# Between two expert layers: where the next layer's statistics, low parts and first rows are made

## The chip, the cores and the metric

One core of one Trainium2 chip runs the whole program. The metric is the device time of one execution in microseconds (us), as a median of several runs. Lines named L... are lines of the kernel before, as the profile names them.

## What is computed

A decaying linear attention over 3,072 tokens makes 384 numbers for each token, and two layers of experts follow. Each layer has 8 experts and sends every token to one of them; the second layer also has a capacity, which drops tokens past it.

```python
logits = x @ w_gate                      # first layer: + modality_bias[modality_id]
e_idx = argmax(logits, 1)                # one expert for each token
gate = 1 / sum(exp(logits - max))        # weight of the chosen expert
out[e_idx == e] = gate * (relu(x @ w1[e]) @ w2[e])
```

Here x is 3072x384, w1[e] is 384x1024 and w2[e] is 1024x384. The second layer routes the first layer's output, so it cannot gather a row before the last token of the first layer has its logits.

## The kernel before

**Places.** Tokens are sorted by expert and cut into places of 128 rows. With this input the first layer has 26 places (0 to 25) and the second 28. Place `j` works in lane `j % 2`, and each lane keeps one expert's matrices: the raw float32 (`raw[l][m]`, m = 0 for w1, 1 for w2), a float16 high part `hi` and a bfloat16 low part `lo`, both scaled by a power of two that follows from the matrix's sum of squares.

**One place.** `fetch` gathers 128 rows by an indirect DMA that GpSimd issues; `turn` transposes them on TensorE. `up` makes the first products (72 matmuls), `hidden` the Relu and its low part, `down` the second products (24 matmuls, the last 8 with the low part of the hidden rows). `record`, `gate` and `chance` make a first-layer row's float16 pair, its second-layer logits and its gate; `store` writes it by GpSimd.

**A new matrix.** ScalarE or VectorE sums its squares in three pieces (`gauge`, L964 on ScalarE, L966 on VectorE), `total` (L970, L971) adds the pieces, `tally` (L907) is a matmul that sums over partitions, `scale` (L917 to L919) makes the power of two, `cast` (L876) or `prep` (L981) makes the high part on ScalarE, and `rest` (L880) or `prep` (L983) the low part on VectorE.

**The order of the work.** Every engine's instructions stand in the order in which the code below issues them; no scheduler moves them. `weave` takes turns between generators. The number of places is known only at run time, so the last steps are nested `If`s on the register `used`, and each has an `Else` with a copy of `drain`, the code for the last place. `drain(25)` runs here. Its bits for place 25 (a new second matrix, a short run of an expert) are not set. An `If` costs the engines in it a branch, and at its end they bring their semaphores to one value; an engine outside it that reads what was written there waits for that end.

**drain(25) before.** It starts with three squares of `raw[0][0]` (`size[0]`), then `up(25)`, `hidden(25)`, then `finish(25)`, whose branch for this input makes three more squares of `raw[0][0]` and two of `raw[1][0]`, woven with the record and gate of earlier places. `down(24)` calls `tally` ahead of its last 8 matmuls (key `2 * KF`), which waits for the end of `finish`. After the second products of 24 and 25 come the last logits, `recall` (it brings each token's choice from places back to token order), `scale` and `cast(0, 0)`, the counting of the second layer's experts (`count_all`, `order`, `sizes`, `places`), and beside it `slow_rest(0, 0)`: four times a multiply and a subtract of 512 columns on GpSimd (L992, L993), which make the low part of two thirds of `raw[0][0]`. Then the engines leave the nest, and `first(1)` compares, multiplies and gathers the first rows of the second layer (`choice` L1055 and L1056, `rows` L1061 to L1065, `check`, `fetch_` L1090, `write`). The flag `redo` is read by four engines (L1702), and `slots(1)` starts with the last third of `raw[0][0]` (`rest(0, 0, 2)`), the table of runs, `turn(0)`, `cast(1, 0)` and `rest(1, 0)`.

Of the kernel before, what the change touches and what calls it, by code (L numbers as in the profile page):

```python
# [11 lines left out]
FP32 = mybir.dt.float32  # L12
# [11 lines left out]
P = 128  # L24
# [75 lines left out]
class Kernel:  # L100
# [774 lines left out]
        for r, h, w in self.thirds(l, m):  # L875
            self.nc.scalar.activation(out=h, in_=r, func=ACTF.Copy, scale=self.wsc[l][m][:, 0:1])  # L876

    def rest(self, l, m, i=0):
        for r, h, w in self.thirds(l, m)[i:]:
            self.nc.vector.scalar_tensor_tensor(  # L880
                out=w, in0=r, scalar=self.wsc[l][m][:, 0:1], in1=h, op0=ALU.mult, op1=ALU.subtract
            )
# [38 lines left out]
    def experts(self, ctx):  # L921
# [34 lines left out]
        def gauge(l, m, i=0, j=3, wait=0, e=S):  # L956

            r, sq = flat(raw[l][m]), self.sq[:, l, m]
            for k in range(wait):
                yield  # L960
            for k in range(i, j):
                x = r[:, k * F:(k + 1) * F]
                if e is S:
                    S.activation(out=junk[:, 0:F], in_=x, func=ACTF.Square, accum_out=sq[:, k:k + 1])  # L964
                else:
                    stt_(out=junk1[:, 0:F], in0=x, scalar=1.0, in1=x, op0=ALU.mult, op1=ALU.mult, accum_out=sq[:, k:k + 1])  # L966
                yield
# [11 lines left out]
        def prep(l, m):  # L979
            for r, h, w in self.thirds(l, m):  # L980
                S.activation(out=h, in_=r, func=ACTF.Copy, scale=wsc[l][m][:, 0:1])  # L981
                yield
                stt_(out=w, in0=r, scalar=wsc[l][m][:, 0:1], in1=h, op0=ALU.mult, op1=ALU.subtract)  # L983

        tmp = [xp.tile([P, F // 2], FP32, name=f"tmp{i}") for i in range(2)]

        def slow_rest(l, m):

            for r, h, w in self.thirds(l, m):
                for i in range(2):  # L990
                    f = slice(i * F // 2, (i + 1) * F // 2)
                    G.tensor_tensor(out=tmp[i], in0=r[:, f], in1=wsc[l][m][:, 0:1].to_broadcast([P, F // 2]), op=ALU.mult)  # L992
                    G.tensor_tensor(out=w[:, f], in0=tmp[i], in1=h[:, f], op=ALU.subtract)  # L993
                    yield

        def inverse(l):
            V.tensor_tensor(out=winv[l], in0=wsc[l][0][:, 1:2], in1=wsc[l][1][:, 1:2], op=ALU.mult)
# [219 lines left out]
        def slots(layer, banks):  # L1217
# [277 lines left out]
            def step(t):  # L1495
# [43 lines left out]
                do(logits, t - 3)  # L1539
                do(turn_rows, t - 2)  # L1540

            def drain(t):
                if layer == 0:
                    size = [gauge((t - 1) % 2, 0), gauge(t % 2, 0, 2), chain(gauge((t - 1) % 2, 1), gauge(t % 2, 1))]
                    weave(islice(size[0], 3))
                up(t)
                hidden(t)
                finish(t, False, (lambda: gauge(t % 2, 0, 0, 2, 3)) if layer == 0 else lambda: ())
                down(t - 1, {2 * KF: tally})
                weigh(t)  # L1550
                renew(t, False)
                load(t, 1)
                if layer == 1:
                    for j in (t - 1, t):
                        if j == t:
                            down(t)
                        weave(out(j))
                        store(j, ob[j % 4][:, 0:D])
                    return
                rec = [record(j) for j in (t - 1, t)]  # L1560
                prob = [chance(j, j > t - 2) for j in range(t - 3, t + 1)]
                slow = slow_rest(0, 0)

                def settled(j):
                    weave(prob[j - t + 3])
                    store(j, ob[j % 4])

                def between():
                    logits(t - 2)
                    logits_plain(t - 1, t)  # L1570

                plain(t - 1)
                turn_out(t - 2)
                logits(t - 3)
                next(rec[0])
                weave(gate(t - 3))
                down(t, {KF: lambda: turn_plain(t - 1), 2 * KF: between})
                next(size[1])
                next(prob[0])
                next(rec[0])  # L1580
                next(rec[0])
                settled(t - 3)
                weave(gate(t - 2), gate(t - 1, plain_logits(t - 1, t)))
                plain(t)
                for l in range(2):
                    total(l, 0)
                weave(rec[0])
                turn_plain(t)
                next(prob[1])
                next(prob[2])  # L1590
                next(rec[1])
                recall(0, t, mk[0], gm, 32)
                tally()
                logits_plain(t, t)
                weave(gate(t, plain_logits(t, t)), prob[1], prob[2])
                store(t - 2, ob[(t - 2) % 4])
                store(t - 1, ob[(t - 1) % 4])
                next(rec[1])
                next(rec[1])
                next(prob[3])  # L1600
                recall(t, t + 1, mk[1], gl, 4)
                for l in range(2):
                    scale(l, 0)
                self.cast(0, 0)
                weave(islice(size[2], 2))
                V.tensor_tensor(out=mk[0], in0=mk[0], in1=mk[1], op=ALU.max)
                V.tensor_tensor(
                    out=self.oh.rearrange("p t e -> p (t e)").rearrange("p (e t) -> p e t", t=NT),
                    in0=C["rev"].rearrange("p (t e) -> p e t", e=NE), in1=mk[0].unsqueeze(1).to_broadcast([P, NE, NT]), op=ALU.is_equal,
                )  # L1610
                self.count_all(pm)
                weave(rec[1])
                weave(islice(slow, 2))
                onehot = self.order(sm, pm, 0, NT, 9, True)
                weave(islice(onehot, 5), sizes(True), prob[3])
                store(t, ob[t % 4])
                weave(islice(slow, 2))
                weave(onehot, places(True))
                weave(size[2])

            def some(n):
                weave(islice(todo, n))
# [3 lines left out]
            if layer == 0:  # L1626
                todo = runs(False)
                choice(SOON, NS)
                rows(SOON, NS)
                write(SOON, NS)  # L1630
                weave(halve(0))
                turn(0)
                weave(halve(1))
            else:
                self.rest(0, 0, 2)
                todo = runs(True)
                some(23)
                load(0, 0)
                turn(0)
                for l in range(2):  # L1640
                    total(l, 1)
                self.cast(1, 0)
                self.rest(1, 0)
                load(1, 0)

# [13 lines left out]
                with c.Else():  # L1659
                    drain(t)  # L1660

            used = reg(2, A, D_, PE, PL, SP)
            last(sure)

        def begin(layer):
# [32 lines left out]
        banks = hs, ys, xtp, otp, lgp  # L1698
        with tc.manual_schedule():
            slots(0, banks)  # L1700
            first(1)
            x = nc.values_load(redo, engines=[ET.Activation, ET.DVE, ET.PE, ET.SP], min_val=0, max_val=1)  # L1702
            with tc.If(x):
                afresh(1)
            slots(1, banks)
# [63 lines left out]
```

## Time and profile before

| | us |
|---|---|
| median of 3 runs (1004.43 to 1015.93) | 1006.25 |
| profiled execution, its own time | 1013.21 |
| its span, first to last instruction | 1011.2 |
| TensorE busy | 784.3 |
| VectorE busy | 713.4 |
| ScalarE busy | 563.7 |
| GpSimd busy | 132.7 |
| TensorE's mean granted clock, share of full speed | 0.872 |

Busy times are sums over the whole program. The change touches some 60 us of it, from the start of the first layer's last place to the second layer's first steps, so what counts is the order of events there: for each engine when an instruction started, how long it sat idle before, and what ended that.

### The profile page before, as it was taken

The page shows a single profiled execution, that of the slowest core. Times are in us where ns is not written, and L with a number is a line of the kernel's source. Part 1 is how long each engine was busy: PE and PEld are TensorE (multiplying, and loading weights), DVE is VectorE, ACT ScalarE, POOL GpSimd, SP SyncE. Part 2 cuts the span into 40 slices and gives each one's busy share as a digit, 9 for nine tenths or more (in the row PEclk, how much of TensorE's full clock was granted, in tenths as well). Part 3 has the DMA queues.
Part 4 walks back from the last instruction along what each step waited for, and adds up shares of the span by engine and source line. Part 5 has one row for each costly group of instructions (what it writes and reads, how often), then busy time and mean ns, then how long its engine had stood idle before and what let it go on. Part 6 is the DMA issues. An engine that isn't in the chain of part 4 may idle for free. (4 is left out here: it accounts for less than half of the span.)

```text
span 1011.2 us, 24545 instructions
## 1 busy us (share of the span) xinstructions
PE 784.3 (78%) x8691; PEld 630.1 (62%) x8691; DVE 713.4 (71%) x2694; ACT 563.7 (56%) x1066; POOL 132.7 (13%) x137
## 2 busy tenths in 40 slices
PE   4343237999899969568799999867177999989994
PEld 2111115888788858456688888745065787768872
DVE  6899998999999897757656656643887556774220
ACT  6455346777656685148655555555656666773221
POOL 1000000000000000200122222110521232222211
PEclk9665557999999968688999999977588999999998
DMA  4211111222222631273261111150064354331110
GB/s 114 106 53 54 58 53 53 81 87 91 75 96 65 238 138 48 52 266 97 68 231 52 51 52 51 35 154 13 26 232 155 104 175 162 109 98 47 49 44 28
DMA packets 49155, 95.06 MB, mean 94 GB/s; under 512 B 14377, under 2 KB 33479, under 8 KB 48913
## 3 DMA queue, kind: packets, MB, share of 16 engines
q1 hardware_dynamic: 36864, 70.89, 20.5%
q0 software_dynamic: 7312, 21.40, 6.9%
q8 instruction: 79, 1.29, 0.6%
q14 instruction: 164, 1.34, 0.4%
q10 hardware_dynamic: 4736, 0.14, 0.3%
HBM read 211.92 MB, written 20.11 MB: 229 GB/s over the span
## 5 line engine op out<-in xcount | busy, mean ns | idle before, releaser
L1278 PE MATMUL hs<-xt,h 128*128 128x128 f16 x2592 | 227.0, 226 | 17.4 <-issue 8.1
L1278 PEld LDWEIGHTS <-h 128*128 128x128 f16 x2592 | 173.0, 101 | 22.8 <-issue 11.7
L1278 PE MATMUL hs<-xt,l 128*128 128x128 f16 x1296 | 149.6, 226 | 4.4 <-DVEq L1439 2.7
L1295 PE MATMUL ys<-cums,hh 128*128 128x384 bf16 (+1 forms) x864 | 150.5, 327 | 0.0
L248 PE MATMUL tp<-sq,ct 128*128 128x432 f32 (+3 forms) x92 | 60.7, 812 | 82.0 <-ACT sq L244 74.1
L1287 DVE SCALAR_TENSOR_TENSOR hl<-hs,hh 128x512 bf16<-128x512 f32 x108 | 70.7, 685 | 68.3 <-ACT hh L1284 67.0
L1295 PEld LDWEIGHTS <-hh 128*128 128x128 f16 x864 | 82.7, 98 | 49.7 <-issue 1.2
L1278 PEld LDWEIGHTS <-l 128*128 128x128 bf16 x1296 | 95.1, 101 | 5.9 <-DVEq L1439 3.3
L1284 ACT ACTIVATE hh<-hs 128x512 f16<-128x512 f32 x108 | 60.7, 589 | 63.3 <-PE hs L1278 59.1
L248 PEld LDWEIGHTS tp<-sq,ct 128*128 128x128 f32 x92 | 24.0, 290 | 114.2 <-ACT sq L244 92.7
L291 DVE TENSOR_TENSOR u<-cums,nz 128x108 f32<-128x108 f32 (+1 forms) x381 | 86.8, 252 | 5.3 <-ACT nz L266 3.4
L1295 PE MATMUL ys<-cums,hl 128*128 128x384 f16 x432 | 84.1, 340 | 0.0
L1090 POOL DMA_INDIRECT xg<-rec,rd x58 | 57.2, 986 | 152.8 <-issue 56.4
L1295 PEld LDWEIGHTS <-hl 128*128 128x128 bf16 x432 | 39.6, 100 | 53.2 <-issue 30.6
L298 DVE TENSOR_TENSOR cums<-u 128x54 f32<-128x54 f32 (+1 forms) x381 | 68.3, 203 | 2.5 <-DVE u L291 0.2
L964 ACT ACTIVATE junk<-cums 128x1024 bf16<-128x1024 f32 x54 | 56.9, 1054 | 20.5 <-DMA cums<-in_w 11.8
L397 PE MATMUL tp<-ct,qk 128*112 128x128 f32 x384 | 60.1, 293 | 6.0 <-DVE qk L391 5.6
L435 PE MATMUL sc<-qT,kT 112*128 112x128 f32 x384 | 53.7, 288 | 2.3 <-ACT qT L400 2.3
L397 PEld LDWEIGHTS tp<-ct,qk 128*112 128x112 f32 x384 | 45.3, 143 | 12.9 <-DVE qk L391 6.6
L1241 POOL DMA_INDIRECT rec<-ob,wr x26 | 26.0, 1002 | 207.7 <-ACTq L1434 137.7
L1011 POOL MEMSET thr<- 1x2 f32 x1 | 0.1, 90 | 397.0 <-PE tp L397 397.0
L435 PEld LDWEIGHTS sc<-qT,kT 112*128 112x128 f32 x384 | 48.8, 200 | 5.0 <-ACT qT L400 3.1
(328 smaller groups left out, 1630.7 us busy)
## 6 DMA issues: line engine op xcount, KB each, us to landing
cums<-in_w SPq DMA_DIRECT2D x112, 1536.0 KB
qkv<-in_qkvt SPq DMA_DIRECT2D x24, 576.0 KB
nz<-in_ain SPq DMA_DIRECT2D x20, 432.0 KB
rec<-xs SPq DMA_DIRECT2D x24, 192.0 KB
out<-zero SPq DMA_DIRECT2D x24, 192.0 KB
xg<-rec,rd POOLq DMA_INDIRECT x58, 3.6
ct<-in_consts POOLq DMA_DIRECT2D x1, 524.5 KB, 5.8
out<-ob,wr POOLq DMA_INDIRECT x28, 3.2
```

The lines of the kernel that those rows point to most:

```text
L248: nc.tensor.matmul(m2, ident, sq[:, r], start=(r == 0), stop=(r == 1))
L291: V.tensor_tensor(out=u, in0=rep(f[:, 1, e - 1, x], S_), in1=four(z[:, 1, k * X + c * w:k * X + (c + 1) * w], s_), op=ALU.mult)
L298: ins = V.tensor_tensor(out=two(f[:, 1, e, x], S_), in0=u[:, :, 0], in1=u[:, :, 1], op=ALU.add)
L397: nc.tensor.transpose(tp[:112, hh * P:(hh + 1) * P], src[:, g * 4 + hh].rearrange("p r d -> p (r d)")[:, :112], ident)
L435: nc.tensor.matmul(sc[:, hh], kT[:, h], qT[:, h], start=True, stop=True)
L964: S.activation(out=junk[:, 0:F], in_=x, func=ACTF.Square, accum_out=sq[:, k:k + 1])
L1090: G.indirect_dma_start(out=xg[j % 3], out_offset=None, in_=self.rec[layer], in_offset=bass.IndirectOffsetOnAxis(ap=rd[:, j:j + 1], axis=0))
L1241: G.indirect_dma_start(out=dst, out_offset=bass.IndirectOffsetOnAxis(ap=wr[:, j:j + 1], axis=0), in_=x, in_offset=None, bounds_check=N - 1 ...
L1278: T.matmul(hs[q][:, g], m[:, c, f], x[:, o + c], start=(n == 0), stop=(n == 3 * KD - 1))
L1284: S.activation(out=hh[j % 2][:, sl], in_=h, func=ACTF.Relu)
L1287: V.scalar_tensor_tensor(out=hl[j % 2][:, sl], in0=h, scalar=0.0, in1=hh[j % 2][:, sl], op0=ALU.max, op1=ALU.subtract)
L1295: T.matmul(y, h[j % 2][:, g], m[:, g], start=(n == 0), stop=(n == 3 * KF - 1))
```

## The change

It edits `drain`, the last place of either layer, and what follows the first layer. `finish`, `weigh` and `renew` are replaced there: `finish_last` has one `If` (a new second matrix) and no squares, and stands behind `up`; a second `If` on the new register `short`, in which TensorE takes part as well, stands behind `down(t - 1)`, which calls no `tally`. The six squares of the two first matrices stand ahead: three behind `finish_last`, three behind `hidden` and ahead of `plain(t - 1)`. `tally` goes into `down(t)` at `KF + 4`, `scale` and `cast(0, 0)` behind it, `rest` of two thirds of `raw[0][0]` goes to VectorE, and `slow_rest` is removed. `cast(1, 0)` moves from the second layer's start to the place where `cast(0, 0)` was, and `first(1)` from behind the nest to the end of each `drain`.

```diff
             def drain(t):
                 if layer == 0:
-                    size = [gauge((t - 1) % 2, 0), gauge(t % 2, 0, 2), chain(gauge((t - 1) % 2, 1), gauge(t % 2, 1))]
-                    weave(islice(size[0], 3))
+                    size = [gauge((t - 1) % 2, 0), gauge(t % 2, 0), chain(gauge((t - 1) % 2, 1), gauge(t % 2, 1))]
                 up(t)
+                finish_last(t)
+                if layer == 0:
+                    weave(size[0])
                 hidden(t)
-                finish(t, False, (lambda: gauge(t % 2, 0, 0, 2, 3)) if layer == 0 else lambda: ())
-                down(t - 1, {2 * KF: tally})
-                weigh(t)
-                renew(t, False)
+                down(t - 1)
+                with when(short, t):
+                    weave(measure(t % 2, 1))
+                    tally()
+                    scale(t % 2, 1)
+                    weave(prep(t % 2, 1))
+                    inverse(t % 2)
                 load(t, 1)
...
+                weave(size[1])
                 plain(t - 1)
...
-                down(t, {KF: lambda: turn_plain(t - 1), 2 * KF: between})
-                next(size[1])
+                for l in range(2):
+                    total(l, 0)
+                down(t, {KF: lambda: turn_plain(t - 1), KF + 4: tally, 2 * KF: between})
                 next(prob[0])
                 next(rec[0])
                 next(rec[0])
-                settled(t - 3)
+                for l in range(2):
+                    scale(l, 0)
+                self.cast(0, 0)
+                self.rest(0, 0, 0, 2)
+                weave(prob[0])
+                store(t - 3, ob[(t - 3) % 4])
                 weave(gate(t - 2), gate(t - 1, plain_logits(t - 1, t)))
                 plain(t)
-                for l in range(2):
-                    total(l, 0)
...
-                tally()
                 logits_plain(t, t)
...
-                for l in range(2):
-                    scale(l, 0)
-                self.cast(0, 0)
-                weave(islice(size[2], 2))
+                self.cast(1, 0)
+                weave(islice(size[2], 1))
...
-                weave(islice(slow, 2))
                 onehot = self.order(sm, pm, 0, NT, 9, True)
                 weave(islice(onehot, 5), sizes(True), prob[3])
                 store(t, ob[t % 4])
-                weave(islice(slow, 2))
                 weave(onehot, places(True))
                 weave(size[2])
+                first(1)
...
+            def finish_last(t):
+                def rows_(*more):
+                    weave(*more, out(t - 2), *([chain(gate(t - 4), chance(t - 4))] if layer == 0 else []))
+                with when(bits[0], t) as c:
+                    rows_(prep(t % 2, 1))
+                    inverse(t % 2)
+                with c.Else():
+                    rows_()
...
-            used = reg(2, A, D_, PE, PL, SP)
+            used, short = reg(2, A, D_, PE, PL, SP), reg(1, A, D_, PE)
```

In the second layer's `slots`, `cast(1, 0)` is left out ahead of `rest(1, 0)`.

TensorE's order in `drain(25)`, kernel before, from the last of the first 16 second products of place 24 on (`hh` is the high part of the hidden rows, `hl` the low part):

```order
L1295 LDWEIGHTS hh_4733
L1295 MATMUL ys_5519<-cums,hh_4733 128x384
L1473 UNCONDITIONAL_BRANCH
L907 LDWEIGHTS onesb
L907 MATMUL m<-sqb,onesb 128x4 [waits DVE_49]
L1295 LDWEIGHTS hl_4735
L1295 MATMUL ys_5519<-cums,hl_4735 128x384
```

The same place with the change, from the last second product of place 24:

```order
L1284 LDWEIGHTS hl_4735
L1284 MATMUL ys_5517<-cums,hl_4735 128x384
L1557 REGISTER_ALU
L1557 COMPARE_AND_BRANCH
L907 LDWEIGHTS onesb
L907 MATMUL m<-sqb,onesb 128x4 [waits DVE_49]
L1557 UNCONDITIONAL_BRANCH
L1557 UNCONDITIONAL_BRANCH [waits PE_49]
L1316 LDWEIGHTS ob_4740 [waits Activation_49]
```

The sum matmul that waits for VectorE no longer stands inside the second products; a branch on `short` stands behind them, and the matmul in it is skipped when the bit is not set.

GpSimd's order at the end of `drain(25)`, kernel before (`rec` is the table of rows that the second layer gathers from):

```order
L992 TENSOR_TENSOR tmp_4760<-cums,wsc_294 128x512
L993 TENSOR_TENSOR l_0_3900<-tmp_4760,h_0_3899 128x512 [waits PE_49,Pool_49]
L1765 ISA [waits DMASW7_49]
L1241 DMA rec_63<-ob_4738,wr 3072x385 [waits DMASW7_49,DMASW6_49,DVE_49]
L992 TENSOR_TENSOR tmp_4759<-cums,wsc_294 128x512
L993 TENSOR_TENSOR l_0_3900<-tmp_4759,h_0_3899 128x512 [waits Activation_49,Pool_49]
```

With the change:

```order
L1230 DMA rec_63<-ob_4737,wr 3072x385 [waits DMASW5_49,DVE_49,Activation_49]
L1770 ISA [waits DMASW7_49]
L1230 DMA rec_63<-ob_4738,wr 3072x385 [waits DMASW6_49,DMASW7_49,DVE_49,Activation_49]
L1770 ISA [waits DMASW0_49]
L1079 DMA xg_4722<-rec_63,rd 128x385 [waits DMASW7_49,DMASW1_49,DVE_49]
L1662 ISA [waits DMASW2_49,DMASW1_49]
L1662 UNCONDITIONAL_BRANCH
```

The multiplies and subtracts are gone, and the second layer's first gather stands ahead of the branch out of the nest.

VectorE's last rows in `drain(25)`, kernel before (`bt` is each token's place):

```order
L824 TENSOR_TENSOR ro<-iota_268,rr 128x384
L1044 TENSOR_TENSOR bt<-bt,ov 128x24 [waits DVE_49]
L1047 TENSOR_SCALAR x_4768<-bt,l_4767 128x24 [waits DVE_49]
L1049 SCALAR_TENSOR_TENSOR bt<-bt,x_4768 128x24 [waits DVE_49]
L1656 UNCONDITIONAL_BRANCH
```

With the change `so` and `sv` of `choice` and the five rows of `check` stand behind the same three rows of `bt`, and then:

```order
L1053 TENSOR_SCALAR gz<-m 128x6 [waits PE_49]
L1054 TENSOR_TENSOR rd<-m,gz 128x6 [waits DVE_49]
L1059 TENSOR_SCALAR em<-m 128x6
L1060 TENSOR_TENSOR em<-em,gz 128x6 [waits DVE_49]
L1061 TENSOR_TENSOR wr<-m,em 128x6 [waits DVE_49]
L1662 UNCONDITIONAL_BRANCH
```

The branch out of the nest stood between `bt` and the rows made from it; now it stands behind them.

## Rows read from the trace of the kernel before

**Rows 1.** Busy time of each engine in one stretch, with clock and DMA.

```profile
core 0: us, PE busy (x) PEld busy (x) DVE busy (x) ACT busy (x) POOL busy (x), PEclk, DMA share, GB/s
...
712.00:727.30 15.30, 0.81 (x3) 0.31 (x3) 14.78 (x30) 13.45 (x25) 11.85 (x10) 0.50 0.11 41
```

**Rows 2.** Timeline, TensorE: start, length, line, operation, [idle before, and what ended it].

```profile
682.34 0.48 PE L1278 MATMUL hs<-xt,h 128*128 128x128 f16 x3 [4.28 <-issue]
...
687.74 2.93 PE L1295 MATMUL ys<-cums,hh 128*128 128x384 f16 x16
696.70 0.16 PE L907 MATMUL m<-sqb,onesb 128*128 128x4 bf16 x1 [6.03 <-DVE ob L1385]
...
704.62 1.46 PE L1295 MATMUL ys<-cums,hl 128*128 128x384 f16 x8
...
707.14 0.75 PE L1404 MATMUL hs<-marks,roT 128*128 128x25 f16 x24
```

**Rows 3.** Timeline, ScalarE, from the hidden rows of place 25 to the counting.

```profile
688.89 1.06 ACT L964 ACTIVATE junk<-cums 128x1024 bf16<-128x1024 f32 x1 [0.31 <-ACT hh L1284]
...
690.77 1.06 ACT L964 ACTIVATE junk<-cums 128x1024 bf16<-128x1024 f32 x1
...
691.95 1.06 ACT L964 ACTIVATE junk<-cums 128x1024 bf16<-128x1024 f32 x1
...
699.48 0.58 ACT L1341 ACTIVATE xs<-ys,fx 128x384 f32<-128x384 f32 x1 [3.41 <-PE ys L1295]
...
706.12 0.58 ACT L1341 ACTIVATE xs<-ys,fx 128x384 f32<-128x384 f32 x1 [1.15 <-PE ys L1295]
...
711.68 3.23 ACT L876 ACTIVATE h<-cums,wsc 128x1024 f16<-128x1024 f32 x3 [0.30 <-DVE wsc L918]
...
718.82 2.73 ACT L818 ACTIVATE ab<-iota,rr 128x128 f16<-128x128 f16 x9 [1.69 <-DVE rr L813]
721.58 1.16 ACT L819 ACTIVATE ro<-ab 128x1152 f16<-128x1152 f16 x1
```

**Rows 4.** Timeline, VectorE, from the last gates to the second layer's start.

```profile
705.00 0.16 DVE L1363 COPY g<-lgp 128x8 f32<-128x8 f32 x1
...
706.08 0.16 DVE L1373 TENSOR_REDUCE marks<-g 128x1 f16<-128x8 f32 x1
...
711.31 0.15 DVE L917 TENSOR_SCALAR wsc<-m 128x1 int32<-128x1 int32 x1
...
711.93 0.17 DVE L1606 TENSOR_TENSOR mk<-mk,mk 128x24 f32<-128x24 f32 x1
...
714.47 0.23 DVE L1019 TENSOR_SCALAR sl<-m,cap 128x8 f32<-128x8 f32 x1 [0.27 <-PE m L1017]
...
714.94 1.50 DVE L1021 TENSOR_SCALAR sl<-sl 128x8 f32<-128x8 f32 x1
...
725.81 1.19 DVE L1047 TENSOR_SCALAR x<-bt,l 128x24 f32<-128x24 f32 x1
...
729.84 0.32 DVE L1055 TENSOR_TENSOR so<-iota,bt 128x144 f16<-128x144 f16 x1 [2.62 <-issue]
...
733.32 1.28 DVE L880 SCALAR_TENSOR_TENSOR l<-cums,wsc,h 128x1024 bf16<-128x1024 f32 x1 [1.12 <-DVEq L1703]
```

**Rows 5.** Timeline, VectorE, the first layer's own counting, GpSimd idle beside it.

```profile
411.00 0.17 DVE L837 TENSOR_SCALAR sl<-sl 128x8 f32<-128x8 f32 x1
...
412.69 0.24 DVE L1047 TENSOR_SCALAR x<-bt,l 128x24 f32<-128x24 f32 x1
```

**Rows 6.** Timeline, GpSimd: the second layer's first gather.

```profile
732.01 1.01 POOL L1090 DMA_INDIRECT xg<-rec,rd  x1 [5.04 <-DVE em L1071]
```

**Rows 7.** Branches on the number of places, TensorE's sequencer: ns min/median/max, times.

```profile
L1656 PEldq COMPARE_BRANCH  x10: 66/76/4822, 646.4 to 993.8; - x10
```

**Rows 8.** Timeline, TensorE, the second layer's first transposes and first sum.

```profile
736.07 0.82 PE L1267 MATMUL xtp<-ident,xg 128*128 128x128 f16 x6 [4.73 <-DVE cb L1143]
...
753.64 0.16 PE L907 MATMUL m<-sqb,onesb 128*128 128x4 bf16 x1 [0.74 <-DVEq L1517]
```

More of the change, by code (lines that the diff above doesn't have):

```diff
@@ L876, in cast, with rest @@
             self.nc.scalar.activation(out=h, in_=r, func=ACTF.Copy, scale=self.wsc[l][m][:, 0:1])
-    def rest(self, l, m, i=0):
-        for r, h, w in self.thirds(l, m)[i:]:
+    def rest(self, l, m, i=0, j=3):
+        for r, h, w in self.thirds(l, m)[i:j]:
             self.nc.vector.scalar_tensor_tensor(
@@ L983, in prep @@
                 stt_(out=w, in0=r, scalar=wsc[l][m][:, 0:1], in1=h, op0=ALU.mult, op1=ALU.subtract)
[L985 to L994, printed above, removed]
         def inverse(l):
@@ L1540, in step @@
                 do(turn_rows, t - 2)
+            def finish_last(t):
[6 more added lines that the diff above has]
+                    rows_()
+                if layer == 1:
+                    store(t - 2, ob[(t - 2) % 4][:, 0:D])
+                else:
+                    store(t - 4, ob[(t - 4) % 4])
             def drain(t):
                 if layer == 0:
-                    size = [gauge((t - 1) % 2, 0), gauge(t % 2, 0, 2), chain(gauge((t - 1) % 2, 1), gauge(t % 2, 1))]
-                    weave(islice(size[0], 3))
+                    size = [gauge((t - 1) % 2, 0), gauge(t % 2, 0), chain(gauge((t - 1) % 2, 1), gauge(t % 2, 1))]
                 up(t)
+                finish_last(t)
+                if layer == 0:
+                    weave(size[0])
                 hidden(t)
-                finish(t, False, (lambda: gauge(t % 2, 0, 0, 2, 3)) if layer == 0 else lambda: ())
-                down(t - 1, {2 * KF: tally})
-                weigh(t)
-                renew(t, False)
+                down(t - 1)
[5 more added lines that the diff above has]
+                    inverse(t % 2)
                 load(t, 1)
@@ L1561, in drain @@
                 prob = [chance(j, j > t - 2) for j in range(t - 3, t + 1)]
[L1562 to L1566, printed above, removed]
                 def between():
@@ L1641, in slots @@
                     total(l, 1)
-                self.cast(1, 0)
                 self.rest(1, 0)
@@ L1700, in experts @@
             slots(0, banks)
-            first(1)
             x = nc.values_load(redo, engines=[ET.Activation, ET.DVE, ET.PE, ET.SP], min_val=0, max_val=1)
```

## The prediction

> **What bounds the kernel now.** Shares of busy time say little here: the change touches some 60 us, so I read the timelines of that stretch, TensorE first, then the engine named in each bracket, then a table by stretch for the part where TensorE does nothing.
>
> TensorE stops three times. In `up(25)` it stands 4.28 us for nothing that the profile names ("issue") [rows 2]; this follows a far branch into `drain(25)`, which stays as it is, so I keep the stop. At 690.67 it stops for 6.03 us in front of `tally` [rows 2]. The bracket names the last VectorE instruction of `finish`, a gate that has nothing to do with the sum: the matmul waits for the end of that `If`, and ScalarE fills it with five squares from 688.89 on, 1.18 us from start to start [rows 3]. So `plain(24)` starts at 699.48, 3.41 us after ScalarE fell idle [rows 3].
>
> From 712 to 727.3 the table shows VectorE busy 14.78 of 15.30 us, GpSimd 11.85, TensorE 0.81 [rows 1]. VectorE alone sets the time there, and its instructions are tiny: 8 columns in 1.50 us at 714.94, 24 columns in 1.19 at 725.81 [rows 4]. In the first layer's counting the same two lines (one on 8 columns, one on 24) took 0.17 and 0.24 [rows 5], with GpSimd idle. GpSimd's low parts hold VectorE up.
>
> At 727.22 VectorE has every token's place, and `choice` starts at 729.84: 2.62 us are the branch out of the nest [rows 4]. Then come 2.2 us to the gather at 732.01 [rows 6] and 4.06 more to the transposes at 736.07 [rows 8]. VectorE's own chain runs on beside that; at 753.64 TensorE waits only 0.74 us for it [rows 8], so both chains are nearly level at the second layer's start.
>
> **The change part by part.** Each term is a shift against the profiled execution.
>
> *Squares and the sum ahead of time: 7.0 gained.* Record, gate and chance of earlier places and three squares now run while `up(25)` does. The stop of 4.28 us leaves ScalarE over 7 us there, and the work is under 7: three squares (3.5) and three short instructions with their VectorE answers. Without that cover each us over it would delay the Relu by one. After the Relu the next three squares start at 688.89 as now and end 3 x 1.18 later, at 692.45. TensorE runs `down(24)` through: 687.74 + 2.93 for 16 matmuls + 1.46 for 8 at full clock (row at 704.62) = 692.1 [rows 2]. `plain(24)` then starts at 692.45, against 699.48. If VectorE or ScalarE enter `drain(25)` late, this shrinks to 5; nothing makes it more than 7.4.
>
> *Casts and two low parts moved onto the path: 2.0 given back.* Before, 7.66 us lie between `plain(24)` and the first `recall` at 707.14 [rows 2, 3]. With the change one square goes from ScalarE's work there (1.2), but `scale` waits for `tally` at `KF + 4`, about 4.2 after `plain(24)`; I take that from the same work in its old place (turning, 12 matmuls, two copies). So the cast starts at 696.65, takes 3.23 [rows 3] and holds `plain(25)` up by some 0.8 (ready near 699.1). VectorE is the later one: first piece of the cast (1.08), two low parts of 1.28 [rows 4], three tiny ones (0.45), the twelve gate instructions (1.24, 705.00 to the end at 706.24 [rows 4]): 696.65 + 5.4 = 702.05. `recall` comes 5.0 earlier instead of 7.0. Bounds: 0.8 (only `plain(25)` counts) to 3.2 (the whole cast does).
>
> *`scale` off the end: 0.6 gained.* Its six instructions, 711.31 to 711.93 [rows 4], now lie under the second products.
>
> *No low parts on GpSimd: 7.3 gained.* From 714.47 to 727.22 are 12.75 us [rows 4]. Eight instructions there are slow; the first and last are the rows at 714.94 and 725.81, and they sum to 9.30. At the length of their like in the first layer's counting, of which two stand in [rows 5], they sum to 1.55. The full difference is 7.75; some of the slow ones already lay beside their neighbours, so I lay the thirty instructions out at quick lengths and get 5.4 us: 7.3 gained. Bounds 5.4 (the two row stores that stay on GpSimd still cost one us each) to 7.75. VectorE then has its places at 727.22 - 5.0 - 0.6 - 7.3 = 714.3.
>
> *`first(1)` ahead of the branch: 0.5 gained.* VectorE still makes the same rows and the same 2.62 us jump, in the other order, and then reads `redo` (1.12 more [rows 4]), so its third low part keeps its distance of 6.1 us to the places. Only the gather gains 2.62; TensorE's own jump now lies behind the rows and takes up to 4.82 [rows 7], which eats one us of it. As the two chains were level within 0.74 [rows 8], VectorE is late next and lets some 0.5 through. Bounds -2 to 2.6.
>
> *Costs: 0.3.* A branch that goes on near by is 0.066 to 0.076 us on TensorE [rows 7]. The one on `short` also waits for TensorE's own last matmul, say 0.2. In the first layer it hides under ScalarE's cast; in the second, where TensorE runs to the end, it shows. The further register read hides behind TensorE's queue, and costs about as much again if it doesn't. `cast(1, 0)` trades places with `cast(0, 0)` and hides beside VectorE.
>
> Sum: 7.0 - 2.0 + 0.6 + 7.3 + 0.5 - 0.3 = 13.1 us. The profiled execution would take 1013.21 - 13.1 = 1000.1. It lay 7 above the median; the work that goes is in every run, so the median goes from 1006.25 to 993.2. That is 1.3%, inside the 2% that a measurement of this kernel can tell from no change.
>
> [...]
>
> [...]
>
> **The rivals.**
>
> *ScalarE becomes the bound.* It used to make four squares behind the one-hot rows (`ab`, 2.73, and 1.16 [rows 3]) under VectorE's slow stretch; now five stand there and the stretch is short. Free of `cast(1, 0)` and a square at 710.8, it ends the one-hot rows at 714.7 and the squares at 720.6, 6.3 behind the places, where the first transposes want their copy 7 behind. If its jump also fetches (2.62 to 4.82), the copy is up to 4 late and the second layer starts 2.5 later than I say: 995.7. For: it had 9 idle us there, now none. Against: TensorE had slack.
>
> *Stores hold VectorE:* 1.9 less gain, 995.1. For: GpSimd multiplies do. Against: they follow VectorE's own results and meet few instructions that run long.
>
> *VectorE's jump gets short,* as `drain` has fewer instructions to pass: 2.6 more, 990.6. Against: nothing says that the target comes near enough.
>
> *Slower: new branches fetch.* TensorE's two branches on `short` (one in each layer) and its jump out of the nest, now behind the rows, each cost 4.82: 14.5, against 13.1 + 0.3 without them, so 1007.3. It decides from 4.5 us a branch. For: 4.82 happened once here. Against: the median is 0.076, and two of the targets are near.
>
> **How the numbers follow.** Forecast 993.2: 0.60. ScalarE bound, 995.7: 0.15. Stores, 995.1: 0.10. Short jump, 990.6: 0.11. Slower, 1007.3: 0.04. With each term at its best (7.4 - 0.8 + 0.6 + 7.75 + 2.6) the gain is 17.5, so 988.7; with each at its worst but the branches (5 - 3.2 + 0.6 + 5.4 - 2 - 0.6) it is 5.2, so 1001.0. Medians of three runs here differ by some us, so the range is 986 to 1002. Faster by over 2% is below 986.1, past the best case by the spread of runs: 0.07. Slower by over 2% needs 20 us that no case has: 0.02. Within 2%: 0.91.
>
> **What would show it.** Right: no wait of TensorE ahead of the last 8 products of place 24; `plain` of place 24 near 692.5 and `recall` 9.6 behind it; no VectorE instruction of 24 columns or fewer over 0.4 us in the counting; GpSimd with indirect DMAs alone there; the places some 13 us earlier, the gather 2 us behind them. Wrong: a stop of several us at the branch on `short`; tiny instructions of one us beside a store; ScalarE's copy of the first rows waiting for ScalarE itself.

## The result and the profile after

The changed kernel takes 992.48 us (median of 4 runs, 991.67 to 994.01) against 1006.14 for the kernel before beside it: 13.7 us less, ratio 0.9852 with a 95% interval of 0.9813 to 0.9891. Run again in another session (`after_again`, below) it is 994.01 against 1007.43, ratio 0.9878 (0.9837 to 0.9919). The forecast was 993.2.

| profiled execution | before | after |
|---|---|---|
| own time, us | 1013.21 | 992.98 |
| span, us | 1011.2 | 991.1 |
| mean granted clock | 0.872 | 0.885 |

The two profiled executions differ by 20.2 us, 6.5 more than the medians, so the stretch of the change is taken apart first. In these rows the changed kernel's line numbers from L986 to L1506 are 11 lower than before (L1295 is now L1284, L1341 is L1330, L1404 is L1393). The first view is TensorE's timeline of the changed kernel; it answers to [rows 2, 8].

```profile
672.78 0.49 PE L1267 MATMUL hs<-xt,h 128*128 128x128 f16 x6 [0.76 <-ACT ot L1317]
...
675.95 0.71 PE L1267 MATMUL hs<-xt,h 128*128 128x128 f16 x5 [1.95 <-issue]
...
680.26 2.76 PE L1284 MATMUL ys<-cums,hh 128*128 128x384 f16 x16
682.86 1.46 PE L1284 MATMUL ys<-cums,hl 128*128 128x384 f16 x8
...
694.45 0.75 PE L1393 MATMUL hs<-marks,roT 128*128 128x25 f16 x24 [1.04 <-DVE marks L1362]
...
712.10 0.82 PE L1256 MATMUL xtp<-ident,xg 128*128 128x128 f16 x6 [3.84 <-DMA xg<-rec,rd]
...
723.93 0.82 PE L1267 MATMUL hs<-xt,h 128*128 128x128 f16 x6 [2.79 <-DVE hl L1276]
...
732.53 0.16 PE L907 MATMUL m<-sqb,onesb 128*128 128x4 bf16 x1 [0.22 <-DVEq L1506]
```

The wait of 6.03 us in front of the last 8 products of place 24 is gone: they follow the first 16 at once. A wait of 2.79 for VectorE has come ahead of `up(1)`. ScalarE's timeline answers to [rows 3]:

```profile
681.56 1.06 ACT L1273 ACTIVATE hh<-hs 128x512 f16<-128x512 f32 x2
682.81 1.06 ACT L964 ACTIVATE junk<-cums 128x1024 bf16<-128x1024 f32 x1 [0.19 <-ACTq L1557]
...
685.17 1.06 ACT L964 ACTIVATE junk<-cums 128x1024 bf16<-128x1024 f32 x1
...
686.23 0.56 ACT L1330 ACTIVATE xs<-ys,fx 128x384 f32<-128x384 f32 x1
...
689.13 3.21 ACT L876 ACTIVATE h<-cums,wsc 128x1024 f16<-128x1024 f32 x3
692.25 0.56 ACT L1330 ACTIVATE xs<-ys,fx 128x384 f32<-128x384 f32 x1
```

Behind the second Relu stand three squares and `plain(24)`, with a branch of 0.19 ahead of them and nothing else, and each starts when the one ahead ends: ScalarE bounds this part. VectorE's timeline answers to [rows 4]:

```profile
701.32 0.23 DVE L1008 TENSOR_SCALAR sl<-m,cap 128x8 f32<-128x8 f32 x1 [0.27 <-PE m L1006]
...
701.78 0.16 DVE L1010 TENSOR_SCALAR sl<-sl 128x8 f32<-128x8 f32 x1
...
706.26 0.24 DVE L1036 TENSOR_SCALAR x<-bt,l 128x24 f32<-128x24 f32 x1
706.53 0.18 DVE L1038 SCALAR_TENSOR_TENSOR bt<-bt,x 128x24 f32<-128x24 f32 x1
...
712.94 1.28 DVE L880 SCALAR_TENSOR_TENSOR l<-cums,wsc,h 128x1024 bf16<-128x1024 f32 x1 [3.81 <-DVEq L1708]
```

The instruction that took 1.50 takes 0.16, the one of 1.19 takes 0.24, as in the first layer's counting. GpSimd, which answers to [rows 6], has only indirect DMAs there (one more store, at 701.53, took 0.97):

```profile
705.06 1.35 POOL L1230 DMA_INDIRECT rec<-ob,wr  x1 [2.56 <-DVE ov L1029]
708.93 0.99 POOL L1079 DMA_INDIRECT xg<-rec,rd  x1 [2.52 <-DVE em L1060]
```

Three more rows of the kernel before give the edges of its stretches, the start of `up(25)`, the second Relu and the last places:

```profile
675.67 0.80 PE L1278 MATMUL hs<-xt,h 128*128 128x128 f16 x6 [2.89 <-issue]
...
687.98 0.60 ACT L1284 ACTIVATE hh<-hs 128x512 f16<-128x512 f32 x1 [3.24 <-PE hs L1278]
...
727.03 0.18 DVE L1049 SCALAR_TENSOR_TENSOR bt<-bt,x 128x24 f32<-128x24 f32 x1
```

Stretch by stretch, from these starts (the second Relu ends at 687.98 + 0.60 before, at 681.56 + 1.06 after):

| stretch | before | after | gained |
|---|---|---|---|
| `up(25)` to the end of its second Relu | 12.91 | 9.84 | 3.07 |
| to `plain(24)` | 10.90 | 3.61 | 7.29 |
| to the first `recall` | 7.66 | 8.22 | -0.56 |
| to `sl` | 7.33 | 6.87 | 0.46 |
| to the last places | 12.74 | 5.39 | 7.35 |
| to the first sum of the second layer (753.64, 732.53) | 26.43 | 25.82 | 0.61 |

The rows sum to 18.22. Another 2.89 lie ahead of them: `up(25)` starts at 675.67 before, behind a first unnamed stop of 2.89, and at 672.78 after, behind a wait of 0.76 for ScalarE. The first row comes from TensorE's unnamed stop, 4.28 before and 1.95 after, and the lower granted clock behind it (0.50 from 682.34 to 687.74 before, a mean of 0.67 from 675.95 to 680.26 after); the runs below show that such a difference needs no change. The others sum to 15.15.

### The profile page after: what moved, and what is told of

The parts are those of the page before. It is cut to its first block, busy times and chain, and to the rows that moved or that the text cites. A ratio compares the mean times of both kernels' runs of the same rounds, so it can differ in the third digit from the quotient of the medians.

```text
span 991.1 us, 24502 instructions
## 1 busy us (share of the span) xinstructions
PE 781.3 (79%) x8689; PEld 628.4 (63%) x8689; DVE 706.5 (71%) x2682; ACT 560.2 (57%) x1060; POOL 124.2 (13%) x129
## 5 line engine op out<-in xcount | busy, mean ns | idle before, releaser
L1284 PE MATMUL ys<-cums,hh 128*128 128x384 bf16 (+1 forms) x864 | 149.4, 326 | 0.1
L248 PE MATMUL tp<-sq,ct 128*128 128x432 f32 (+3 forms) x92 | 57.8, 778 | 81.0 <-ACT sq L244 61.3
L1284 PEld LDWEIGHTS <-hh 128*128 128x128 f16 x864 | 82.1, 98 | 49.2 <-issue 0.5
L248 PEld LDWEIGHTS tp<-sq,ct 128*128 128x128 f32 x92 | 23.1, 279 | 111.6 <-ACT sq L244 92.8
L1284 PE MATMUL ys<-cums,hl 128*128 128x384 f16 x432 | 83.9, 339 | 0.0
L1284 PEld LDWEIGHTS <-hl 128*128 128x128 bf16 x432 | 39.7, 100 | 48.8 <-issue 26.3
L964 ACT ACTIVATE junk<-cums 128x1024 bf16<-128x1024 f32 x51 | 53.7, 1054 | 18.8 <-DMA cums<-in_w 13.2
```

Source lines behind the costliest of these rows:

```text
L248: nc.tensor.matmul(m2, ident, sq[:, r], start=(r == 0), stop=(r == 1))
L1284: T.matmul(y, h[j % 2][:, g], m[:, g], start=(n == 0), stop=(n == 3 * KF - 1))
```

## The experiments

**The kernel before, once more.**

> The kernel before, unchanged, once more with a profile. My sum took TensorE's unnamed stop of 4.28 us in up(25) as a fixed cost of the far branch into the last place; the changed kernel shows 1.95 us there. If the stop belongs to the place of the code, it is again 4.0 to 4.5 us here, and the time of the profiled execution is near 1006. If it differs from one execution to the next, it is anywhere between 1.9 and 4.5, and the 10.4 us that the changed kernel wins from the start of up(25) to plain(24) are then 7 to 8 of the change and 2 to 3 of luck in the one profile. VectorE's jump behind the places should be 2.6 again and the slow tiny instructions of the counting again 1.0 to 1.5 each.

```profile
673.96 0.50 PE L1278 MATMUL hs<-xt,h 128*128 128x128 f16 x6 [2.25 <-issue]
...
680.07 0.48 PE L1278 MATMUL hs<-xt,h 128*128 128x128 f16 x3 [4.78 <-issue]
...
694.43 0.16 PE L907 MATMUL m<-sqb,onesb 128*128 128x4 bf16 x1 [6.08 <-DVE ob L1385]
```

The execution took 1009.93, where 17 others of this kernel have a median of 1004.75. The stop is 4.78 and the wait at the sum 6.08 again; the counting takes 12.71. So the stop looked like a property of the code, until the next run.

**The kernel before without GpSimd's low parts,** twice.

```diff
-                weave(islice(slow, 2))
                 onehot = self.order(sm, pm, 0, NT, 9, True)
...
-                weave(islice(slow, 2))
                 weave(onehot, places(True))
```

> The kernel before without the two low parts that GpSimd makes in the last place's counting (two of the three thirds of the low part of the second layer's first matrix in slot 0 are left out, and nothing is put in their place). Theory: they hold VectorE's tiny instructions up, so the stretch from sl (L1019) to the last places goes from 12.75 to 5.4 us, no instruction of 24 columns or fewer there takes over 0.4 us, and the time falls by 7.3 to about 998.8. Rival 1, the two row stores on GpSimd hold VectorE too: the stretch is 7.3, the time 1000.7. Rival 2, the counting waits for ScalarE's one-hot rows or squares instead: the stretch shrinks but the second layer's gather or first copy comes no earlier, time within 3 us of before.

> The kernel before without GpSimd's two low parts, a second time, as its trace gave back 7.4 us in the counting (5.30 instead of 12.7) and its median only 4.0. If the whole of it arrives, the median is near 998 and the first four us were a draw; if VectorE or TensorE's stops take a part of it back in most executions, the median is again 1000 to 1001.5 and the trace shows where (an entry stop over 1, a stop in up(25) over 1.6, or a jump behind the places over 2.6).

TensorE and VectorE of the first of the two:

```profile
674.56 0.49 PE L1278 MATMUL hs<-xt,h 128*128 128x128 f16 x6 [1.03 <-ACT ot L1328]
...
677.50 0.48 PE L1278 MATMUL hs<-xt,h 128*128 128x128 f16 x3 [1.61 <-issue]
...
690.67 0.17 PE L907 MATMUL m<-sqb,onesb 128*128 128x4 bf16 x1 [6.16 <-DVE ob L1385]
```

```profile
707.66 0.23 DVE L1019 TENSOR_SCALAR sl<-m,cap 128x8 f32<-128x8 f32 x1 [0.27 <-PE m L1017]
...
712.78 0.18 DVE L1049 SCALAR_TENSOR_TENSOR bt<-bt,x 128x24 f32<-128x24 f32 x1
```

The counting takes 5.30 us (5.35 in the second), 7.4 less, and no tiny instruction there is over 0.4: the low parts were the cause in the trace. The medians give 1000.75 against 1004.75 (ratio 0.9959, 0.9936 to 0.9982) and 999.75 against 1007.43 (0.9922, 0.9894 to 0.9950), 4.0 and 7.7 us. Two sessions of one kernel lie that far apart, and 7.4 is inside the second interval only. The other reading is as useful: with no change ahead of the counting, the stop in `up(25)` is 1.61 here (1.85 in the second) instead of 4.28 and 4.78. It differs between executions, so the median of before need not contain the long one. A small part of the 7.4 is lost again within the trace: the first sum of the second layer comes 27.04 and 27.28 behind the places, 26.43 before.

**A weight load moved.** The real load of 1.5 MB issued at 674.17 waits behind a tiny transfer from the hidden rows of place 25.

```diff
...
+                if t > sure:
+                    nc.sync.dma_start(out=self.late, in_=hh[t % 2][0:1, 0, 0:8])
+                    load(t - 1, 1)
...
```

> The kernel before, with one weight load moved: the second matrix of slot 0 (1.5 MB, issued by SP at 674.17, DMA at 330 to 465 GB/s from 676.4 to 680.0) now waits behind a tiny transfer that reads the hidden rows of place 25, so it starts behind up(25). Theory: TensorE's stop of 4.28 us in up(25) (4.78 in the second profile) is its code waiting beside that load; in the profiles where the stop began ahead of the load's full rate it took 1.61 to 2.63. Without the load beside it the stop is under 2.0, the clock comes back inside up(25), and from the start of up(25) to plain(24) it takes 18.9 or less instead of 23.3 to 23.8; the profiled execution falls by 4 to 6, the median of the runs by 0 to 5, as the runs without a profile may have had the short stop already. Rival: the stop belongs to the code alone and stays at 4.0 to 4.8, time unchanged. Second rival: the load only moves into the next stretch and holds up another fetch there, time unchanged with a stop elsewhere.

> The changed kernel with the same weight load moved behind up(25). Theory: the stop of 1.95 us in up(25) (1.89 and 2.63 in two kernels like it) falls to 1.6 or less, ScalarE and VectorE enter the last place no later; gain 0.3 to 1.5, time 991 to 992. Rival: the load now runs beside the second products and the branch on the short last place, and a fetch there takes 2 or more, time 993 or above.

The load now goes out at 678.92 (before) and 687.78 (changed), behind `up(25)`. The stops are 1.71 and 1.84, the times 1005.80 against 1005.81 (ratio 0.9994, 0.9961 to 1.0026) and 993.88 (0.9864, 0.9827 to 0.9901). Neither kernel got faster, and stops of 1.6 to 2 come with the load beside them or without, so it is not their cause.

It does go with the two of over 4 us. The traces list DMA packets by queue, and a queue of kind `instruction`, q8, moves packets of 16 KB. In all 14 stops, those of the runs below too, one such packet lands 1.1 to 1.6 us before the stop ends: TensorE looks to be waiting for its code, though the profile doesn't say whose code q8 brings. In the two long stops (packets at 679.26 and 677.30, 3.59 and 3.34 behind the start of `up(25)`) 770 and 747 of the load's 1,024 packets had started ahead of it. In the 11 others in this `up(25)` at most 18 had, and the packet started 0.57 to 1.20 behind. That the load held the packet up rests on this order alone; no run put the load there on purpose.

**The low parts back on GpSimd.**

```diff
...
-                self.rest(0, 0, 0, 2)
+                slow = slow_rest(0, 0)
...
+                weave(islice(slow, 2))
                 onehot = self.order(sm, pm, 0, NT, 9, True)
...
+                weave(islice(slow, 2))
                 weave(onehot, places(True))
```

> The changed kernel with the two low parts back on GpSimd, in the places that they had before, and gone from VectorE behind the first cast. Theory: sl to the last places goes from 5.39 back to about 12.7 us (+7.3); plain(24) to recall falls from 8.22 by what the two low parts cost VectorE there, 1.5 to 2.5; together 4.8 to 5.8 slower than the changed kernel, so 997.3 to 998.3. Rival: the low parts cost nothing where VectorE makes them (ScalarE's cast and plain(25) end last there), so plain(24) to recall stays at 8.2 and the time is 999.8. Second rival: what slowed VectorE before was the cast of slot 0 and the squares beside it, not GpSimd; then the stretch stays under 7 and the time within 2 us of 992.5.

Busy time from `sl` to the last places, first of this run, then of the changed kernel:

```profile
core 0: us, PE busy (x) PEld busy (x) DVE busy (x) ACT busy (x) POOL busy (x), PEclk, DMA share, GB/s
702.77:714.21 11.44, 0.00 (x0) 0.10 (x1) 11.34 (x23) 9.12 (x20) 10.28 (x10) 0.50 0.09 35
```

```profile
701.32:706.71 5.39, 0.00 (x0) 0.00 (x0) 5.25 (x23) 5.36 (x14) 2.33 (x2) 0.50 0.10 37
```

The same 23 instructions of VectorE take 11.34 us beside ten of GpSimd and 5.25 beside two. `plain(24)` to `recall` is 7.37 instead of 8.22. So in the trace the low parts cost 6.05 on GpSimd and 0.85 on VectorE. The time is 998.58 (0.9919, 0.9891 to 0.9947); the next run, on the same chip, shows 991.54. The theory holds. Why it is 11.44 and not 12.7 is open; in this run the last subtract, from 714.05 on, ends behind the places (714.21), while in the kernel before the last one (725.81, 1.15 long) ends ahead of them (727.21). Two of GpSimd's rows in the kernel before show how it holds VectorE up:

```profile
715.34 1.06 POOL L992 TENSOR_TENSOR tmp<-cums,wsc 128x512 f32<-128x512 f32 x1
716.48 1.18 POOL L993 TENSOR_TENSOR l<-tmp,h 128x512 bf16<-128x512 f32 x1
```

VectorE's instruction of 1.50 us ends at 716.44, GpSimd's multiply at 716.40; its next slow one (716.57, 1.11 long) ends at 717.68, GpSimd's subtract at 717.66. Both last until GpSimd's instruction is over.

**The next rows behind the branch again** (`first(1)` moved back).

> The changed kernel with the second layer's next rows found behind the branch out of the nest again, as before. Theory: the gather comes 2.6 us later behind the last places (4.8 instead of 2.2), but VectorE, which makes the same rows and the same jump, ends its work ahead of up(1) at the same distance, so the first sum of step 0 comes only 0.5 to 0.6 later and the time is about 993.0. Rival: the gather's path decides, and the time is 2.6 higher, 995.1. Second rival: the jump is shorter or longer for its new place, so that the time moves the other way by up to 2 us.

```profile
716.92 0.82 PE L1256 MATMUL xtp<-ident,xg 128*128 128x128 f16 x6 [4.50 <-DVE fl L1134]
...
726.32 0.50 PE L1267 MATMUL hs<-xt,h 128*128 128x128 f16 x6 [1.03 <-DVE hl L1276]
...
734.36 0.17 PE L907 MATMUL m<-sqb,onesb 128*128 128x4 bf16 x1 [0.74 <-DVEq L1506]
```

The gather comes 5.23 behind the places instead of 2.22, but `up(1)` waits 1.03 for VectorE instead of 2.79, and the first sum comes 26.50 behind the places instead of 25.82. The time, 991.54 (0.9858, 0.9829 to 0.9887), is that of the changed kernel: the gather was moved by 3.0, the end by 0.7, and no median shows it.

**Squares, sum and casts alone** (the edits of the two runs above together).

> The changed kernel with the low parts back on GpSimd and the next rows back behind the branch, so only the squares and the sum ahead of time, the moved casts and the branches remain of the change. Theory: from the start of up(25) to plain(24) 13 to 14 us (changed kernel 13.45, kernel before without low parts 18.89), plain(24) to recall 7.4, sl to the last places 11.4 to 12.7, gather 4.8 to 5.2 behind them; time 5 to 6 under the kernel before, 999 to 1000. Rival: as forecast, 7.0 less what the cast costs, so 998 or less. Second rival: the wait that went (6 us in front of the sum) was covered by something else in the runs without a profile, time within 3 of before.

997.32 against 1005.81 (0.9907, 0.9872 to 0.9942): 8.5 us, more than the 5 to 6 expected, though its interval (5.8 to 12.9) takes them in. `up(25)` to `plain(24)` is 14.40, `recall` 7.37 behind, the counting 11.47. Some 1.3 of the 8.5 are the counting, 12.74 before.

**The changed kernel without VectorE's two low parts,** and the changed kernel once more.

> The changed kernel without the two low parts that VectorE makes behind the first cast (two thirds of the low part of the second layer's first matrix in slot 0 are left out). Theory: they cost 0.85 to 1.2 us on the path (plain(24) to recall is 8.22 and 8.57 with them, 7.37 in both kernels that have them on GpSimd), so plain(24) to recall is 7.3 to 7.4 and the time about 1 less than the changed kernel's. Rival, as forecast: ScalarE's cast and VectorE's low parts both count there and 2.0 comes back, recall 6.2 to 6.5 behind plain(24). Second rival: all 2.48 us of VectorE's work count.

> The changed kernel, unchanged, once more with a profile and beside the same executions of the kernel before. Expected 991.5 to 993.5, a ratio of 0.986 to 0.989; sl to the last places 5.2 to 5.5 us, plain(24) to recall 8.0 to 8.6; the stop in up(25) anywhere from 1.6 to 3, as it differs between executions. If ScalarE's jump out of the nest takes 2.7 us here (0.51 in the first profile, 2.68 in the run with earlier casts), the second layer's first copy is late by 2 and the first layer's end is bound by ScalarE, as the first rival of the forecast has it; if it is again about 0.5, it isn't.

Without them `plain(24)` to `recall` is 7.38 (8.57 with them beside it, 8.22 in the first profile): 0.8 to 1.2 us come back, not 2.0. The time is 992.17 (0.9852, 0.9812 to 0.9892) against 994.01, a difference inside the noise. ScalarE's first copy in `after_again`:

```profile
710.44 0.80 ACT L1257 COPY xt<-xtp 128x768 f16<-128x768 f16 x1 [0.49 <-PE xtp L1256]
```

It is TensorE's transposes that end its wait, as in the first profile (0.51): ScalarE doesn't bound the layer's end.

**More squares and casts ahead.**

```diff
-                    size = [gauge((t - 1) % 2, 0), gauge(t % 2, 0), ...
+                    size = [gauge((t - 1) % 2, 0), gauge(t % 2, 0, e=V), ...
...
-                down(t - 1)
+                down(t - 1, {2 * KF: tally} if layer == 0 else {})
...
                 plain(t - 1)
+                for l in range(2):
+                    scale(l, 0)
+                self.cast(0, 0, 0, 1)
...
```

> The changed kernel with more moved the same way: the three squares of slot 1's first matrix on VectorE instead of ScalarE while up(25) runs, one square ahead of the records, the sum inside place 24's second products, and the first two pieces of the cast and their low parts under place 25's second products, the third piece in ScalarE's idle 2.75 us behind recall. Theory: ScalarE bounds the stretch from up(25) to plain(24) now (it is busy 5.71 of 6.00 us from 680 to 686 and 6.00 from 686 to 692), so plain(24) starts 1.8 earlier, at TensorE's end of place 24, and the first recall 3 to 4 earlier than now; time 2.5 to 4 under the changed kernel, 988.5 to 990. Rival: TensorE's own products bound it, so the squares are hidden either way and nothing moves by more than 1 us. Second rival: the sum waits for VectorE's squares inside place 24's products and costs 1 to 3.

ScalarE, then VectorE:

```profile
677.66 0.58 ACT L1300 ACTIVATE junk<-ys,fx 128x384 bf16<-128x384 f32 x1 [2.60 <-issue]
...
715.36 0.80 ACT L1257 COPY xt<-xtp 128x768 f16<-128x768 f16 x1 [2.68 <-ACTq L1712]
```

```profile
715.33 1.28 DVE L880 SCALAR_TENSOR_TENSOR l<-cums,wsc,h 128x1024 bf16<-128x1024 f32 x1 [6.11 <-ACTq L1712]
```

A miss: 996.86 (0.9903, 0.9866 to 0.9941). The records started 2.60 late for nothing that the profile names, VectorE's squares came behind them, and TensorE's sum waited 0.76. `recall` is 0.66 earlier behind `plain(24)`, which is no earlier (13.84). Then ScalarE's jump took 2.68 (in the changed kernel ScalarE was idle there for 0.51, until TensorE's transposes ended), VectorE waited for it at the end of the `If`, 6.11 instead of 3.81, and `up(1)` came 2.1 later behind the first transposes (13.91, changed kernel 11.83): the first rival's mechanism, in another kernel.

**Two more branches.**

```diff
                 with when(short, t):
...
+                for _ in range(2):
+                    with when(short, t):
+                        tally()
```

> The changed kernel with two more branches on the bit for a short last place, in each layer, on TensorE (each skips one sum matmul). Theory: a branch that goes on near by costs TensorE 0.07 to 0.2 us; in the first layer it hides under ScalarE's squares, in the second it shows, together 0.2 to 0.5, time 992.5 to 993.5. Rival, the slower case of the forecast: each such branch makes TensorE stop for its code, 1.6 to 4.8 us, so 2 to 10 us more in each layer, 996 or above.

`up(27)` of the second layer, its last place, then the way from place 26's second products to place 27's, in this run:

```profile
968.51:978.22 9.71, 6.53 (x72) 6.34 (x73) 0.69 (x1) 0.60 (x1) 0.99 (x1) 0.65 0.08 26
```

```profile
968.51 0.22 PE L1267 MATMUL hs<-xt,h 128*128 128x128 f16 x1 [0.95 <-ACT ob L1293]
971.90 0.71 PE L1267 MATMUL hs<-xt,h 128*128 128x128 f16 x5 [3.17 <-issue]
...
980.82 1.46 PE L1284 MATMUL ys<-cums,hl 128*128 128x384 f16 x8
983.26 2.76 PE L1284 MATMUL ys<-cums,hh 128*128 128x384 f16 x16 [0.97 <-PEq L1564]
```

The same two places in the changed kernel:

```profile
964.95:968.97 4.02, 4.02 (x72) 4.01 (x73) 0.69 (x1) 0.85 (x2) 0.99 (x1) 1.00 0.17 59
```

```profile
971.57 1.46 PE L1284 MATMUL ys<-cums,hl 128*128 128x384 f16 x8
973.18 2.76 PE L1284 MATMUL ys<-cums,hh 128*128 128x384 f16 x16
```

999.07 (0.9926, 0.9898 to 0.9955), 5 to 6.6 us more than the changed kernel, the rival's size but not by its mechanism. TensorE stands 0.98 between the two places' products (983.26 - 982.28) instead of 0.15 (973.18 - 973.03): 0.42 a branch. The larger part is a new stop of 3.17 in the second layer's `up(27)`, ahead of that layer's added branches, and a lower granted clock (a mean of 0.65 instead of 1.00; six matmuls behind the stop take 0.85, where they take 0.50 in the changed kernel): the same 72 matmuls take 9.71 instead of 4.02. Another 1.4 stand at the second layer's start, where the first sum comes 27.25 behind the places instead of 25.82, with ScalarE's jump at 1.96 and VectorE's wait for it at 5.25. In the first layer the stop in `up(25)` is gone at the same time. That did not help there:

```profile
673.93 0.49 PE L1267 MATMUL hs<-xt,h 128*128 128x128 f16 x6 [0.93 <-ACT ot L1317]
...
677.95 2.76 PE L1284 MATMUL ys<-cums,hh 128*128 128x384 f16 x16
...
688.43 0.55 PE L1336 MATMUL xtp<-ct,xs 128*128 128x128 f32 x3 [2.99 <-ACT xs L1330]
```

TensorE comes through without a stop and waits 2.99 for ScalarE's `plain(24)`, which starts 13.89 behind `up(25)`, as with stops of 1.95 (13.45) and 2.63 (13.76).

## Why the prediction was right, and where it was not

*Squares and the sum, 7.0: right in mechanism.* From the second Relu to `plain(24)` the trace gives 7.29. The sum's wait is gone, and three squares alone stand between.

*The step that failed is "so I keep the stop".* The stop is 1.6 to 2.9 in every profile but the two of before, and gone in one. From `up(25)` to `plain(24)` the kernel before takes 23.3 and 23.8 with long stops, and 18.9, 20.0 and 20.2 with short ones (the two runs without low parts and the one with the load moved, where no compute ahead of the counting was changed). The changed kernel takes 13.45 and 13.43 in its two profiles, and 13.9 in the run where the stop was gone, as ScalarE bounds it. So the two profiled executions of before hold some 4 us that its other executions need not have, and they lie 5 to 7 above the medians.

ScalarE's work ahead of the first Relu was under 7, as forecast (6.52, from 675.04 to 681.56). But without the long stop TensorE's first products all ended by 680.4, so in this profile ScalarE's work, and not TensorE, set the time of both Relus: the cover that the forecast counted on was missing. Against short stops the squares and the sum are worth 5.4 to 6.7 from `up(25)` on, not 7.0.

*Casts and low parts on the path, 2.0: mis-sized, 0.56,* and 0.8 to 1.2 for the low parts alone. The step was "`scale` waits for `tally` at `KF + 4`, about 4.2 after `plain(24)`": the cast started 2.9 behind it (689.13 - 686.23). Place 25's first 8 second products stood behind `plain(24)` before (700.09, 2.25 long); now they lie ahead of it (684.96, 1.46 long).

*`scale` off the end, 0.6:* 0.46. *No low parts on GpSimd, 7.3: right* in the trace, 7.35 here and 7.4 alone. Beside the changed kernel's earlier cast they would cost 6.05. The times, 4.0 and 7.7 alone, agree with this no better than they do with each other.

The second rival, stores that hold VectorE for 1.9 (an estimate; no row of before shows it), comes to under 0.5 here: beside the store at 705.06 no tiny instruction took longer, beside the one at 701.53 two took 0.36 and 0.28 (0.43 and 0.35 in `after_again`) instead of 0.17. The store at 705.06 itself took 1.35, the gather behind it 0.99. What made that store longer stays open.

*`first(1)` ahead of the branch, 0.5: right,* 0.61 in the trace and 0.7 by its own run, and for the reason given: VectorE is late next. VectorE's jump did not get short, as the third rival had it: its low part starts 6.23 behind the places, 6.11 before. The places come 20.5 earlier in the profile, the gather 23.1.

*The branch, 0.3: right as a sum,* 0.15 in the changed kernel, 0.42 for each further one. The slower rival, branches that fetch, did not happen. Its price exists: the stop of 3.17 came to a place ahead of the added branches, 1.3 behind the landing of a q8 packet, so it looks like code that came late there, and why there is open. In the kernel before, six of TensorE's ten branches at L1656 took 0.066 to 0.078 us and four 3.40 to 4.82, the longest at 670.7 on the way into `drain(25)`; what set their lengths apart, a fetch of code or something else, no run shows.

The first rival, ScalarE as the bound, did not happen in the changed kernel, but came with a few more rows in `early_casts` and `two_more_branches`.

The terms as the trace has them sum to 15.15; with 5.4 to 6.7 for the first they sum to 13.3 to 14.6, and the medians show 13.7 and 13.4. That the median's executions had the short stop is inferred, no trace of the unchanged kernel shows one. The close hit, 992.5 against 993.2, is in part luck: the first term was 0.3 to 1.6 too large, the casts' cost 1.4 too large, and these offset each other.

## What to carry to other kernels

A stop without a named cause is not a constant: look at it in a second profile before it enters a sum, and ask whether the changed kernel's bound would even see it. Keep multiplies off GpSimd while VectorE runs a chain of tiny instructions: here 2.5 us of VectorE's own time replaced 6 to 7. An edit that only adds a few cheap instructions can move an unnamed stop to a place without cover, so a profile's last stretch is worth a look even when nothing was changed there.

## What was not expected of the hardware

- TensorE's unnamed stop moves with a few rows of code: two skipped branches took the stop out of the first layer's `up(25)` (0 instead of 1.95) and put 3.17 us into the second's `up(27)`, where 72 matmuls went from 4.02 us at a granted clock of 1.00 to 9.71 at a mean of 0.65, so 2.5 of the 5.7 us lie behind the stop, where six matmuls take 0.85 instead of 0.50. One profile shows it, and the medians, 5 to 6.6 apart, bear it out.
- Each of 14 such stops ended 1.1 to 1.6 us after a 16 KB packet of an instruction queue had landed, and the two long ones are those in which a weight load's packets had started ahead of it.
- VectorE's wait of 6.11 us at the branch on `redo` ended with ScalarE's jump there of 2.68 (5.25 and 1.96 with two more branches; 3.81 in the changed kernel, where no jump of ScalarE's shows): one engine's jump was paid for by another.
